# Guard loads five steps ahead, squares on two engines, and head 0 prepared ahead of attention, in a fused gated block with its gradients

## The chip, the cores and the metric

The kernel runs on one core of a Trainium2 chip. The metric is the device time of one execution in microseconds (us); lower is better. Executions of one kernel agree within a few tenths of a per cent. A ratio to the kernel before comes from runs on the same chip, in alternating rounds. The experiments were run in several sets of rounds, on more than one chip, and the median of before lay between 5482 and 5495 us; so between two changed kernels of different sets the ratios are the better comparison.

Abbreviations in the profile: PE is TensorE's matmuls, PEld its weight loads (they overlap PE), DVE is VectorE, ACT is ScalarE, POOL is GpSimd, SP is SyncE. "SPq" is the queue of transfers issued from SP. L324 is line 324 of that kernel's own file; line numbers of before and after differ for the same statement.

## The reference, cut to what matters

```python
def forward(A_x, A_k_cache, A_v_cache, A_wq, A_wo, B_w_gate, B_w_up, B_w_down):
    xn = layernorm(A_x)                                   # 1 x 2048 x 576
    q = (xn @ A_wq) -> 32 heads of 128                    # K, V: 32 x 2048 x 128, given
    p = softmax(q k^T * 128 ** -0.5)
    s = (p v) -> 2048 x 4096, @ A_wo
    g, u = xn @ B_w_gate, xn @ B_w_up                     # 2048 x 4608
    b = (sigmoid(g) * u) @ B_w_down                       # 2048 x 576
    return A_x + s * silu(b)

out, vjp = jax.vjp(forward, ...)
return (out, *vjp(grad_out))                              # and eight gradients; all bfloat16
```

The kernel runs, in this order: layer norm with the gate and up products (`h = sigmoid(g) * u`, stored to DRAM), the w_down product (h is read back transposed), attention forward and backward for 32 heads, and the weight and input gradients. One more thing runs beside gate and up: the *guard*. It sums the squares of all of K and of wq (84 pieces, 21.5 MB read) to bound the largest score, and sets a flag. The flag selects between two versions of attention, one without the row maximum (`fast`) and one with it. In all runs here the fast one is taken.

## The kernel before

The guard: each piece is loaded by SP into one of two buffers of the pool `gd`, and squared by ACT. One piece is issued for each step of the gate/up loop, from the second column group on.

```python
gp = tc.alloc_tile_pool(name="gd", bufs=2)
...
def guard_k(h, hf):
    v = gp.tile([P, GQ], bf, name="gk")
    src = A_k_cache[0, h].rearrange("(p t) d -> p t d", t=NT)[:, hf * NT // 2:(hf + 1) * NT // 2, :]
    nc.sync.dma_start(v[:].rearrange("p (t d) -> p t d", d=P), src)
    nc.scalar.activation(v[:], v[:], AF.Square, accum_out=ksq[:, 2 * h + hf:2 * h + hf + 1])
...                                             # guard_w: the same for pieces of wq
def guard_end():
    ...                                         # sums by partition, into gm
    nc.sync.dma_start(gd_d[0:1, :].rearrange("o p -> p o"), gm[:, 0:1])
    nc.sync.dma_start(gd_d[1:2, :].rearrange("o p -> p o"), gm[:, 1:2])
    gr = gp.tile([1, 2, P], f32, name="gr", bufs=1)
    nc.sync.dma_start(gr[:], gd_d[:, :].rearrange("(o a) p -> o a p", o=1))
    ...                                         # DVE: gs and flag_i from gr
```

The gate/up loop; a step is one pass of the inner loop. `x_all` holds x, then the normalised x, and is dead once it is stored to `xn_d` in the first column group.

```python
for grp in range(NFC // GRP):                   # 3 groups of 3 column chunks of 512
    for st in range(NT):                        # 16 row tiles of 128
        if grp == 0 and st + LA < NT:
            ln_tile(st + LA)
        if grp == 0 and st == NT - 1:
            nc.gpsimd.dma_start(xn_d[:, :].rearrange("(t p) d -> p t d", p=P), xn_st[:])
            ...
        for c in range(GRP):
            ...                                 # 5 + 5 matmuls of 512 columns: g_ps, u_ps
            nc.scalar.activation(a_row[:, cs], g_ps[:], AF.Sigmoid)
            oma = tmpp.tile([P, FCH], bf, name="oma")
            nc.scalar.activation(oma[:], g_ps[:], AF.Sigmoid, scale=-1.0)
            if grp > 0 and guards:
                guards.pop(0)()
            nc.vector.tensor_tensor(h_row[:, cs], u_ps[:], a_row[:, cs], op=ALU.mult)
            nc.vector.tensor_tensor(b_row[:, cs], h_row[:, cs], oma[:], op=ALU.mult)
        ...                                     # GpSimd stores h_row, a_row, b_row to DRAM
```

The w_down stage begins with a transposing read of h, and attention begins by allocating the head tiles, then the score slabs, then the transposed tiles.

```python
for st in ...:
    hT_st = hp.tile([P, FT, P], bf, name="hT_st")
    nc.sync.dma_start_transpose(hT_st[:], h_d[srows, :])
    ...                                         # matmuls with wd_sb, then silu and its derivative

def attention(fast):
    wst = pool("wst", 1)                        # wq_h, woT_h (two each) and wo_h
    ld2, ld1 = pool("ld2", 2), pool("ld1", 1)   # Kn (two), Vn, KT, VT, QT, dOT, dOn, Qn
    slabp = pool("slab", SLABS)                 # 18 slabs "Pq", 128 x 2048 bf16
    wsneg = None if fast else pool("wsneg", 3)
    wpt = pool("wpt", 7 if fast else 4)         # transposed slabs "PT" and "dST"
    wt, stg = pool("wt", 2), pool("stg", 2)
    ...
    def prep_loads(h):
        ...
        hs.wo_h = wst.tile([P, D], bf, name="wo_h")      # 576 x 2 bytes in each partition
        ...
    def transpose_slab(hs, qt, name):
        T = wpt.tile([P, NT, P], bf, name=name, tag="PT")
        nc.sync.dma_start_transpose(T[:], hs.slabs[qt][:])
        return T
    ...
    heads[0] = prep_loads(0)                    # all of head 0's preparation, before any score
    prep_kt(heads[0]); prep_wot(heads[0]); ...
```

Each head has 16 query tiles, and each of them is transposed twice (P for P·V, dS for dQ): 1024 transfers of 512 KB by way of the DMA engines.

Of the kernel before, what the change touches and what calls it, by code (L numbers as in the profile page):

```python
# [13 lines left out]
P = 128  # L14
# [81 lines left out]
def kernel(  # L96
# [67 lines left out]

    px = tc.alloc_tile_pool(name="px", bufs=1)
# [3 lines left out]
    with tc.tile_pool(name="pa", bufs=1) as pa:  # L169
# [7 lines left out]
        NGW = -(-HD // GQ)  # L177

        def guard_k(h, hf):
            v = gp.tile([P, GQ], bf, name="gk")  # L180
            src = A_k_cache[0, h].rearrange("(p t) d -> p t d", t=NT)[:, hf * NT // 2:(hf + 1) * NT // 2, :]
            nc.sync.dma_start(v[:].rearrange("p (t d) -> p t d", d=P), src)
            nc.scalar.activation(v[:], v[:], AF.Square, accum_out=ksq[:, 2 * h + hf:2 * h + hf + 1])

        def guard_w(i, c):
            d0, kd = dts[i]
            n = min(GQ, HD - c * GQ)
            v = gp.tile([P, GQ], bf, name="gk")
            nc.sync.dma_start(v[:kd, :n], A_wq[d0:d0 + kd, c * GQ:c * GQ + n])
            nc.scalar.activation(v[:kd, :n], v[:kd, :n], AF.Square, accum_out=wsq[:kd, NGW * i + c:NGW * i + c + 1])  # L190

# [17 lines left out]
        guards = [lambda h=h, hf=hf: guard_k(h, hf) for h in range(H) for hf in range(2)] + [lambda i=i, hf=hf: guard_w(i, hf) for i in range(DT) for hf in range(NGW)]  # L209
        with tc.tile_pool(name="a1w", bufs=1) as wp:  # L210
            a0x = tc.alloc_tile_pool(name="a0x", bufs=1)
            x_all = a0x.tile([P, NT, D], bf, name="x_all")
# [20 lines left out]
            with tc.tile_pool(name="a0", bufs=3) as sb0, tc.tile_pool(name="a0ps", bufs=2, space=PSUM) as ps0, \  # L233
# [23 lines left out]
                for grp in range(NFC // GRP):  # L257
                    for st in range(NT):
# [9 lines left out]
                        for c in range(GRP):  # L268
# [14 lines left out]
                            if grp > 0 and guards:  # L283
                                guards.pop(0)()
# [6 lines left out]
            a0x.release()  # L291
        for g_ in guards:
            g_()
        guard_end()
        gp.release()
# [4 lines left out]
        with tc.tile_pool(name="a2h", bufs=4) as hp, \  # L300
# [4 lines left out]
            for sg in range(NT // SG):  # L305
# [7 lines left out]
                for sl in range(SG):  # L313
                    st = sg * SG + sl
                    srows = slice(st * P, (st + 1) * P)
                    hT_st = hp.tile([P, FT, P], bf, name="hT_st")
                    nc.sync.dma_start_transpose(hT_st[:], h_d[srows, :])
# [21 lines left out]

            for (t_, sl_, st_) in pend2:  # L340
                transpose_to(nc, pst, t_[:, sl_, :], D, dsT, st_ * P, ident, alt)

    NTH = max(1, NT // 2)
    GPI = -(-NT // NTH)
    SKEW = 5
    G4 = min(4, NT)

    def attention(fast):
        with ExitStack() as es:
            def pool(name, bufs, **kw):  # L350
                return es.enter_context(tc.tile_pool(name=("f_" if fast else "g_") + name, bufs=bufs, **kw))
            wst = pool("wst", 1)
            ld2, ld1 = pool("ld2", 2), pool("ld1", 1)
# [9 lines left out]
            wqs = [wst.tile([P, DT, P], bf, name=f"wq_h{b}") for b in range(2)]  # L363
            woTs = [wst.tile([P, DT, P], bf, name=f"woT_h{b}") for b in range(2)]
            for t_ in wqs + woTs:
                zpad(t_)

            def acc_tile(dtype=f32):
                if dtype == f32:
                    return ps_acc.tile([P, 4, P], f32, name="acc", tag="acc")  # L370
                return ps_acc.tile([P, 8, P], bf, name="acct", tag="acc")

            def pe_transpose_blocks(src_fn, lo, hi, dst_fn, eng):
                for g in range(lo, hi, 8):
                    n = min(8, hi - g)
                    pt = acc_tile(bf)
                    for j in range(n):
                        nc.tensor.transpose(pt[:, j, :], src_fn(g + j), ident[:])
                    alt.copy(dst_fn(g, n), pt[:, :n, :], eng=eng)

            class HeadState:
                pass

            def prep_loads(h):
                hs = HeadState()
                hs.h = h
                hs.wq, hs.woT = wqs[h % 2], woTs[h % 2]
                hcols = slice(h * P, (h + 1) * P)
                nf = DT - 1 if KPAD else DT
                if nf:  # L390
                    nc.gpsimd.dma_start(hs.wq[:, :nf, :], A_wq[:nf * P, hcols].rearrange("(i p) c -> p i c", p=P))
                if KPAD:
                    nc.gpsimd.dma_start(hs.wq[:kd_last, nf, :], A_wq[nf * P:, hcols])
                hs.wo_h = wst.tile([P, D], bf, name="wo_h")
                nc.gpsimd.dma_start(hs.wo_h[:], A_wo[hcols, :])
                hs.Kn = ld2.tile([P, NT, P], bf, name="Kn")
                nc.gpsimd.dma_start(hs.Kn[:], A_k_cache[0, h].rearrange("(p t) d -> p t d", t=NT))
                hs.Vn = ld1.tile([P, NT, P], bf, name="Vn")
                nc.gpsimd.dma_start(hs.Vn[:], A_v_cache[0, h].rearrange("(p t) d -> p t d", t=NT))
                hs.rs_all = hstat.tile([P, NT], f32, name="rs_all")  # L400
                hs.rinv_all = hstat.tile([P, NT], f32, name="rinv_all")
                hs.delta = hstat.tile([P, NT], f32, name="delta")
                hs.negdelta = hstat.tile([P, NT], f32, name="negdelta")
                hs.rsc = hstat.tile([P, NT], f32, name="rsc")
                hs.slabs = [None] * NT
                hs.PT = [None] * NT
                hs.dST = [None] * NT
                return hs

            def prep_kt(hs):  # L410
                hs.KT = ld1.tile([P, S], bf, name="KT")
                KTv = hs.KT[:].rearrange("p (t q) -> p t q", q=P)
                pe_transpose_blocks(lambda j: hs.Kn[:, j, :], 0, NT, lambda g, n: KTv[:, g:g + n, :], "s")

            def prep_vt(hs):
                hs.VT = ld1.tile([P, S], bf, name="VT")
                VTv = hs.VT[:].rearrange("p (t q) -> p t q", q=P)
                pe_transpose_blocks(lambda j: hs.Vn[:, j, :], 0, NT, lambda g, n: VTv[:, g:g + n, :], "v")

            def prep_wot(hs):  # L420
                pt = acc_tile(bf)
                for i, (d0, kd) in enumerate(dts):
                    nc.tensor.transpose(pt[:kd, i, :], hs.wo_h[:, d0:d0 + kd], ident[:])
                nf = DT - 1 if KPAD else DT
                if nf:
                    alt.copy(hs.woT[:, :nf, :], pt[:, :nf, :], eng="s")
                if KPAD:
                    alt.copy(hs.woT[:kd_last, nf, :], pt[:kd_last, nf, :], eng="s")

            def gen_T(w, srcT, dst, sc, eng):  # L430
                acc = acc_tile()
                av = acc[:].rearrange("p a b -> p (a b)")
                cs = slice(sc * CH, (sc + 1) * CH)
                for i, (d0, kd) in enumerate(dts):
                    kk = kfull(i, kd)
                    nc.tensor.matmul(av[:, :CH], lhsT=w[:kk, i, :], rhs=srcT[:kk, i, cs], start=(i == 0), stop=(i == DT - 1))  # L436
                alt.copy(dst[:, cs], av[:, :CH], eng=eng)

            def prep_qt(hs, sc):
                if sc == 0:  # L440
                    hs.QT = ld1.tile([P, S], bf, name="QT")
                gen_T(hs.wq, xnT, hs.QT, sc, "s")

            def prep_dot(hs, sc):
                if sc == 0:
                    hs.dOT = ld1.tile([P, S], bf, name="dOT")
                    hs.dOn = ld1.tile([P, NT, P], bf, name="dOn")
                gen_T(hs.woT, dsT, hs.dOT, sc, "v")

            def prep_don(hs, sc):  # L450
                pe_transpose_blocks(lambda j: hs.dOT[:, j * P:(j + 1) * P], sc * nb, (sc + 1) * nb,
                                    lambda g, n: hs.dOn[:, g:g + n, :], "v")

            def prep_qn(hs):
                hs.Qn = ld1.tile([P, NT, P], bf, name="Qn")
                pe_transpose_blocks(lambda j: hs.QT[:, j * P:(j + 1) * P], 0, NT, lambda g, n: hs.Qn[:, g:g + n, :], "v")
# [18 lines left out]
            def main1(hs, qt, hf):  # L475
                if hf == 0:
                    hs.slabs[qt] = slabp.tile([P, S], bf, name="Pq")
                    hs.rsp = stat.tile([P, NHF], f32, name="rsp")
                    hs.nm = stat.tile([P, NHF], f32, name="nm")
                    hs.snegs = []  # L480
# [101 lines left out]
            NSC = S // CH  # L582
            nb = CH // P

# [29 lines left out]
            def plan(h):  # L614
# [3 lines left out]
                if h:  # L618
                    put(pl + q(skew + 1), 0, lambda: heads.__setitem__(h, prep_loads(h)))
# [27 lines left out]

            heads[0] = prep_loads(0)
            prep_kt(heads[0])
            prep_wot(heads[0])  # L650
            for sc in range(NSC):
                prep_qt(heads[0], sc)
# [278 lines left out]
```

## Time and profile before

Three runs had a median of 5479.09 us (5476.99 to 5485.14). The profiled execution was a slower one of the kernel: its span is 5498.0 us. In this table and the later ones a stage ends where its last instruction starts, and the gradients at the end of the span.

| stage (profile) | ends at, us | length, us |
|---|---|---|
| layer norm, gate and up, guard: to the last of its matmuls | 417.8 | 417.8 |
| gap to the first w_down matmul | 435.4 | 17.6 |
| w_down | 585.5 | 150.1 |
| gap to the first score matmul | 606.2 | 20.7 |
| attention: to the last sum of dK (DVE, behind its last product) | 3903.0 | 3296.8 |
| gradients | 5498.0 | 1595.0 |

This is the page of the kernel before: span, busy time of each engine with its share of the span and its instruction count, and the DMA queues with packets, MB and the share of 16 engines' time.

```profile
span 5498.0 us, 129982 instructions
...
PE 5095.5 (93%) x54343; PEld 3654.3 (66%) x55220; DVE 2497.0 (45%) x5692; ACT 2695.0 (49%) x4794; POOL 1420.1 (26%) x2361
...
q1 hardware_dynamic: 2637890, 764.83, 76.0%
```

PE leads with 93%, so what can be gained is PE's idle time and little else. The average hides the stages. The next lines are the windows view of before: stretch in us, its length, each engine's busy us with instruction counts, the granted TensorE clock (PEclk, 1.00 is full speed), the DMA share and GB/s.

```profile
core 0: us, PE busy (x) PEld busy (x) DVE busy (x) ACT busy (x) POOL busy (x), PEclk, DMA share, GB/s
155.00:291.00 136.00, 108.31 (x475) 47.63 (x485) 54.21 (x98) 100.17 (x195) 26.54 (x50) 0.99 0.66 234
372.00:419.00 47.00, 45.95 (x210) 20.74 (x212) 24.15 (x43) 23.67 (x44) 11.95 (x23) 1.00 0.43 178
700.00:3700.00 3000.00, 2841.93 (x36169) 2259.92 (x36751) 1703.53 (x3814) 1950.09 (x3299) 931.93 (x1600) 1.00 1.14 198
```

With guards (first line) PE is busy 108 of 136 us; without them (second line) 46 of 47. In attention (third line) the DMA share is 1.14. A share above 1 says that the recorded packet times sum to more than the engines' time, so they overlap; I take it as engines that have little time to spare.

The waits view of before, first from 120 to 340 us, then from 340 to 420: who waited for whom, us in total, times, longest.

```profile
ACT gk L183 <- DMA gk<-in_A_k_cache_dram: 46.8, 23, 3.7
PE g_ps L276 <- ACT oma L282: 47.8, 24, 7.5
...
DVE gs L203 <- DMA gr<-gd_d: 10.6, 1, 10.6
PE u_ps L279 <- DVE h_row L285: 8.9, 1, 8.9
```

ACT's squares stand for the guard's loads, the sigmoids stand behind the squares in ACT's order, and PE stands for the sigmoids. Later DVE stands 10.6 us for the guard's sum to return from DRAM, and PE 8.9 us behind DVE. The two gaps are in the timeline view of PE in before (start, length, line, operation; in brackets the idle time ahead and what ended it):

```profile
435.44 17.77 PE L324 MATMUL acc<-wd_sb,hT_st 128*128 128x512 bf16 x125 [17.29 <-DMA hT_st<-h_d]
...
598.11 1.86 PE L378 MATMUL acct<-ident,Kn 128*128 128x128 bf16 x16 [7.48 <-DMA Kn<-in_A_k_cache_dram]
...
606.24 0.59 PE L466 MATMUL sp<-KT,QT 128*128 128x512 bf16 x2
```

```profile
q1 hardware_dynamic: 1942260, 489.69, 100.3%
q0 software_dynamic: 34432, 100.08, 13.3%
```

PE stands 65.6 + 25.6 = 91.2 us of attention for transposed tiles that have not landed. Each packet of the transposing queue takes 3000 us x 16 x 1.003 / 1942260 = 24.8 ns.

### The profile page before, as it was taken

The page shows a single profiled execution, that of the slowest core. Times are in us where ns is not written, and L with a number is a line of the kernel's source. Part 1 is how long each engine was busy: PE and PEld are TensorE (multiplying, and loading weights), DVE is VectorE, ACT ScalarE, POOL GpSimd, SP SyncE. Part 2 cuts the span into 40 slices and gives each one's busy share as a digit, 9 for nine tenths or more (in the row PEclk, how much of TensorE's full clock was granted, in tenths as well). Part 3 has the DMA queues.
Part 4 walks back from the last instruction along what each step waited for, and adds up shares of the span by engine and source line. Part 5 has one row for each costly group of instructions (what it writes and reads, how often), then busy time and mean ns, then how long its engine had stood idle before and what let it go on. Part 6 is the DMA issues. An engine that isn't in the chain of part 4 may idle for free. (4 is left out here: it accounts for less than half of the span.)

```text
span 5498.0 us, 129982 instructions
## 1 busy us (share of the span) xinstructions
PE 5095.5 (93%) x54343; PEld 3654.3 (66%) x55220; DVE 2497.0 (45%) x5692; ACT 2695.0 (49%) x4794; POOL 1420.1 (26%) x2361
## 2 busy tenths in 40 slices
PE   8878899999999999999999999999789999899999
PEld 3334577777777777777777777777557777644454
DVE  4443455655655555655556555555333333210011
ACT  7751466666666666666666666666222222100000
POOL 2212323323333233333233233223112222211000
PEclk9999999999999999999999999999999999999999
DMA  7658799999999999999999999999945455674865
GB/s 282 235 187 194 155 199 189 204 196 201 200 200 198 200 198 193 200 205 199 201 200 199 188 199 198 200 198 189 236 143 195 167 174 180 199 219 120 172 146 111
DMA packets 2721787, 1053.95 MB, mean 192 GB/s; under 512 B 2521937, under 2 KB 2642386, under 8 KB 2719138
## 3 DMA queue, kind: packets, MB, share of 16 engines
q1 hardware_dynamic: 2637890, 764.83, 76.0%
q0 software_dynamic: 83296, 280.64, 16.6%
q8 instruction: 434, 7.11, 0.5%
q14 instruction: 167, 1.37, 0.1%
HBM read 213.91 MB, written 201.00 MB: 75 GB/s over the span
## 5 line engine op out<-in xcount | busy, mean ns | idle before, releaser
L484 ACT ACTIVATE Pq<-sp 128x1024 bf16<-128x1024 f32 x1024 | 1048.1, 1024 | 328.2 <-PE sp L466 205.5
L570 PEld LDWEIGHTS <-Pq 128*128 128x128 bf16 x16384 | 1002.5, 98 | 241.2 <-issue 2.1
L542 ACT ACTIVATE t<-dp,negdelta 128x1024 bf16<-128x1024 f32 x512 | 571.5, 1116 | 278.9 <-POOL negdelta L524 160.7
L538 DVE SCALAR_TENSOR_TENSOR Pq<-dp,delta,Pq 128x1024 bf16<-128x1024 f32 x512 | 655.0, 1279 | 58.1 <-PE acc L510 56.4
L510 PE MATMUL acc<-Kn,dST 128*128 128x128 bf16 x8192 | 554.0, 220 | 69.3 <-DMA dST<-Pq 65.6
L510 PEld LDWEIGHTS <-PT 128*128 128x128 bf16 x8192 | 498.8, 98 | 156.4 <-DMA PT<-Pq 47.8
L543 DVE TENSOR_TENSOR Pq<-t,Pq 128x1024 bf16<-128x1024 bf16 x512 | 419.1, 819 | 398.1 <-ACT t L542 394.9
L535 PE MATMUL dp<-VT,dOT 128*128 128x512 bf16 x1728 | 541.5, 380 | 53.7 <-DVE Pq L538 53.6
L510 PEld LDWEIGHTS <-dST 128*128 128x128 bf16 x8192 | 490.4, 98 | 140.3 <-DMA dST<-Pq 85.7
L510 PE MATMUL acc<-Vn,PT 128*128 128x128 bf16 x8192 | 547.8, 219 | 33.0 <-DMA PT<-Pq 25.6
L570 PE MATMUL acc<-dOn,Pq 128*128 128x128 bf16 x8192 | 546.5, 219 | 10.3 <-DVE o_n L50 0.2
L466 PE MATMUL sp<-KT,QT 128*128 128x512 bf16 x1762 | 547.7, 379 | 1.2 <-ACT Pq L484 1.2
L570 PE MATMUL acc<-Qn,Pq 128*128 128x128 bf16 x8192 | 541.3, 219 | 3.4
L499 POOL TENSOR_SCALAR dOn<-dOn,rinv_all 128x128 bf16<-128x128 bf16 x512 | 313.9, 613 | 612.0 <-DVE rinv_all L472 502.9
L552 ACT ACTIVATE dq_n<-acc,rsc 128x128 bf16<-128x128 f32 x512 | 188.3, 368 | 401.8 <-PE acc L510 401.8
L800 PEld LDWEIGHTS <-xn_all 128*128 128x128 bf16 (+1 forms) x2880 | 281.5, 100 | 40.3 <-issue 11.1
L50 DVE TENSOR_SCALAR o_n<-acc,rinv_all 128x128 bf16<-128x128 f32 x352 | 123.5, 351 | 299.3 <-PE acc L510 299.3
L580 POOL DMA_DIRECT2D out_dram<-kvo x256 | 148.9, 582 | 406.3 <-DVE kvo L579 404.0
L276 PE MATMUL g_ps<-wg_sb,xnT 128*128 128x512 bf16 x694 | 185.8, 392 | 59.8 <-ACT oma L282 50.2
L504 POOL DMA_DIRECT2D dq_d<-dq_n x128 | 98.3, 768 | 497.5 <-ACT dq_n L552 479.7
L535 PEld LDWEIGHTS <-dOT 128*128 128x128 bf16 x2048 | 164.3, 98 | 83.0 <-issue 61.0
L881 ACT ACTIVATE dxn<-acc 128x512 f32<-128x512 f32 (+1 forms) x32 | 12.7, 411 | 420.8 <-PE acc L872 420.8
(182 smaller groups left out, 7163.6 us busy)
## 6 DMA issues: line engine op xcount, KB each, us to landing
out_dram<-kvo POOLq DMA_DIRECT2D x256, 128.0 KB, 4.6
h_d<-h_row POOLq DMA_DIRECT2D x48, 384.0 KB, 4.3
a_d<-a_row POOLq DMA_DIRECT2D x48, 384.0 KB, 3.1
b_d<-b_row POOLq DMA_DIRECT2D x48, 384.0 KB, 5.2
a_blk<-a_d SPq DMA_DIRECT2D x18, 1024.0 KB, 5.8
b_blk<-b_d SPq DMA_DIRECT2D x18, 1024.0 KB, 18.9
h_blk<-h_d POOLq DMA_DIRECT2D x18, 1024.0 KB, 11.4
du_d<-du_blk POOLq DMA_DIRECT2D x18, 1024.0 KB, 9.1
```

The costliest lines, as they stand in the source:

```text
L276: nc.tensor.matmul(g_ps[:], lhsT=xnT[:kk, i, srows], rhs=wg_sb[:kk, i, fs], start=(i == 0), stop=(i == DT - 1))
L466: nc.tensor.matmul(sp[:, c * CH:(c + 1) * CH], lhsT=hs.QT[:, qt * P:(qt + 1) * P], rhs=hs.KT[:, hf * HW_ + c * CH: hf * HW_ + (c + 1) * CH ...
L484: nc.scalar.activation(Pq[:, hsl], sp[:], AF.Exp, scale=SCALE, accum_out=hs.rsp[:, hf:hf + 1])
L499: nc.gpsimd.tensor_scalar(hs.dOn[:, qt, :], hs.dOn[:, qt, :], hs.rinv_all[:, qt:qt + 1], None, op0=ALU.mult)
L510: nc.tensor.matmul(hs.acc[:, 0, :], lhsT=T[:, kt, :], rhs=rhs[:, kt, :], start=(kt == 0), stop=(kt == NT - 1))
L535: nc.tensor.matmul(dp[:, c * CH:(c + 1) * CH], lhsT=hs.dOT[:, qt * P:(qt + 1) * P], rhs=hs.VT[:, hf * HW_ + c * CH: hf * HW_ + (c + 1) * C ...
L538: nc.vector.scalar_tensor_tensor(Pq[:, hsl], dp[:], hs.delta[:, qt:qt + 1], Pq[:, hsl], op0=ALU.subtract, op1=ALU.mult)
L542: nc.scalar.activation(t[:], dp[:], AF.Identity, bias=hs.negdelta[:, qt:qt + 1], scale=1.0)
L543: nc.vector.tensor_tensor(Pq[:, hsl], t[:], Pq[:, hsl], op=ALU.mult)
L552: nc.scalar.activation(hs.dq_n[:, qt % G4, :], hs.acc[:, 0, :], AF.Copy, scale=hs.rsc[:, qt:qt + 1])
L570: nc.tensor.matmul(self.tile[:, j, :], lhsT=self.slabs[qt][:, kt * P:(kt + 1) * P], rhs=self.rhs[:, qt, :], start=(qt == self.lo), stop=(q ...
L800: nc.tensor.matmul(acc[:kd, :], lhsT=xn_all[:, st, d0:d0 + kd], rhs=blk_[:, st, :], start=(st == 0), stop=(st == NT - 1))
```

## The change

Its intent: give the guard's loads a long lead, share the squares between ACT and DVE, and take the two gaps away.

- The guard's pieces go to nine slots of the dead x buffer. A piece is loaded five guard steps before it is squared. Odd pieces are squared on ACT and even ones on DVE.
- The first two transposed h tiles also go to the x buffer, so that they are loaded before the last matmuls of gate and up free their pool.
- Head 0's loads, K^T, wo^T and Q^T are done in the w_down stage. For that the head tiles move out of attention's pools into the pool `pdT`, which lies on the right-hand side of SBUF and lives longer. `hT_st` has three buffers in place of four.

```diff
-        def guard_k(h, hf):
-            v = gp.tile([P, GQ], bf, name="gk")
-            ...
-            nc.scalar.activation(v[:], v[:], AF.Square, accum_out=ksq[:, 2 * h + hf:2 * h + hf + 1])
+        NGS = NT * D // GQ
+        GLA = min(5, NGS - 1)
+        ...
+        def piece_view(k):
+            kind, i, c = pieces[k]
+            v = x_flat[0][:, (k % NGS) * GQ:(k % NGS + 1) * GQ]
+            ...
+        def guard_square(k):
+            v, acc = piece_view(k)
+            if k % 2:
+                nc.scalar.activation(v, v, AF.Square, accum_out=acc)
+            else:
+                nc.vector.scalar_tensor_tensor(v, v, 1.0, v, op0=ALU.mult, op1=ALU.mult, accum_out=acc)
+        ...
+        def guard_step():
+            k = gk[0]
+            if k < len(pieces):
+                guard_load(k)
+            if 0 <= k - GLA < len(pieces):
+                guard_square(k - GLA)
+            gk[0] += 1
 ...
-                            if grp > 0 and guards:
-                                guards.pop(0)()
+                            if grp > 0:
+                                guard_step()
 ...
+            for st in range(NHV):                          # NHV is 2
+                nc.sync.dma_start_transpose(hT_first[st], h_d[st * P:(st + 1) * P, :])
 ...
+        wqs = [pdT.tile([P, DT, P], bf, name=f"wq_h{b}") for b in range(2)]
+        woTs = [pdT.tile([P, DT, P], bf, name=f"woT_h{b}") for b in range(2)]
+        ...
+        wo_h = pdT.tile([P, D], bf, name="wo_h")
+        Kns = [pdT.tile([P, NT, P], bf, name=f"Kn{b}") for b in range(2)]
+        Vn, dOn, Qn = [pdT.tile([P, NT, P], bf, name=nm) for nm in ("Vn", "dOn", "Qn")]
+        KT, VT, QT, dOT = [pdT.tile([P, S], bf, name=nm) for nm in ("KT", "VT", "QT", "dOT")]
+        heads_pre[0] = prep_loads(0)
-        with tc.tile_pool(name="a2h", bufs=4) as hp, \
+        with tc.tile_pool(name="a2h", bufs=3) as hp, \
 ...                                                       # at the end of the w_down stage:
+            prep_kt(heads_pre[0])
+            prep_wot(heads_pre[0])
+            for sc in range(S // CH):
+                prep_qt(heads_pre[0], sc)
 ...                                                       # in attention:
-            wst = pool("wst", 1)
-            ld2, ld1 = pool("ld2", 2), pool("ld1", 1)
             slabp = pool("slab", SLABS)
 ...
-            heads[0] = prep_loads(0)
-            prep_kt(heads[0])
-            prep_wot(heads[0])
-            ...
+            heads[0] = start_head(0)                       # takes what was prepared
```

## The prediction

> **What bounds the kernel now.** PE is busy 93% (page, part 1). Stages (windows view): gate/up 0–419 us, h·w_down 436–586, attention 608 to about 4120, gradients. Only the first two and the seams behind them change.
>
> Gate/up in the timeline: a step (5+5 matmuls of 512 columns) takes 2.16 us at 372–419, where no guard runs. At 155–291 one step with one guard takes 2.8 us (8.4 us a row tile): in the waits, ACT's squares stand 46.8 us for guard loads (two buffers), and the sigmoids behind them hold PE (47.8 us). PE is busy 108 of 136 us there, DMA 66%. The guard's round trip through DRAM then holds DVE 10.6 us and PE 8.9. Seams: PE waits 17.3 us for the first transposed h tile (418–435.4), and from the last w_down matmul (585.7) to the first score matmul (606.2) 20.5 us pass, 7.5 of them a wait for head 0's K.
>
> **The change.** The 84 guard pieces keep their bytes (21 MB). The load lookahead goes from 2 buffers to 9 slots of x, half the squares move from ACT (1.06 us + 0.19) to DVE (I estimate 1.2 us from the 0.76 us of a 576-column scalar_tensor_tensor). Removed from the seams: the h wait, head 0's loads and the idle behind them. Head 0's preparation moves before the branch, not saved. Otherwise attention's built instruction order is the same on PE, DVE, ACT and SP.
>
> The built order decides more than the source: all 84 pieces in 37 steps (2.27 a step, 42 on each engine), starting at step 39 (about 122 us), and then 68 steps without guards. There PE needs 80 us, ACT about 80, DVE about 90 (estimates from durations). DMA needs more: 21.2 MB of guards at 327 GB/s plus 14.2 MB of stores at 411 GB/s (rates: bytes over share of each queue in the DMA view) make 100 us of all 16 engines. The Trainium skill ("Trainium Kernel Development and Optimization", Key Constraints) says that the queues all run on the same 16 engines; here the two queues' shares do add up, 36.6% + 27.7% at 120–340 us. So I expect this burst DMA-bound: about 105 us.
>
> **Sum** (estimates). Gate/up: 122 + 3 (first guard load waits for the store of x, 10.9 us to landing) + 105 + 68 × 2.16 + 6 (the guard's DRAM round trip is still in DVE's order 2–3 steps after its start) = about 383 instead of 419: −36. h seam: 17 to about 1: −16. Attention seam: KT, woT and Q (about 7 us at warm clock) run while the last ds tile is made, first score matmul about 10 us after the last w_down matmul: −10. Together −62: **5417 us**, 8 in 10: 5392 to 5444. Chances: faster by over 2% 0.03, within 2% 0.96, slower 0.01.
>
> **What would show it.** Gate/up ends near 383; DMA share over 0.9 for some 100 us from about 125; DVE waiting on the guard's returning load 6–10 us; first w_down matmul within 2 us of the last gate/up step; first score matmul 10 us after the last w_down matmul; attention and later stages within 5 us of before.
>
> **What would make it wrong.** DMA carries more than 340 GB/s in the burst: up to 25 us better. Guard waits on two in-order engines stall PE more, or stores pile up: 20 us worse. The head-0 loads delay the third h tile. Attention, 64% of the span, shifting.

## More of the kernel before

In attention two groups of the page carry the waits (L510: busy us, mean ns, then idle us just before, and its main releaser), and the DMA view from 700 to 3700 us gives the queue that carries the transposes (q1: packets, MB, share):

```profile
L510 PE MATMUL acc<-Kn,dST 128*128 128x128 bf16 x8192 | 554.0, 220 | 69.3 <-DMA dST<-Pq 65.6
...
L510 PE MATMUL acc<-Vn,PT 128*128 128x128 bf16 x8192 | 547.8, 219 | 33.0 <-DMA PT<-Pq 25.6
```

## The result, and the profile after

| | median, us | runs |
|---|---|---|
| before | 5482.11 (5476.99 to 5492.95) | 4 |
| after | 5346.53 (5345.28 to 5347.66) | 4 |

The ratio is 0.975, with a 95% interval of 0.9733 to 0.9767: faster by 2.5%. Here and below a ratio is the mean time of one kernel's fast runs over that of the other's of the same rounds, so it is not quite the ratio of the medians quoted. The gain of 136 us is more than twice the 62 us of the prediction, and the time lies below its range.

| stage (both profiles) | before, us | after, us | difference | predicted |
|---|---|---|---|---|
| gate and up | 417.8 | 378.6 | -39.2 | -36 |
| gap to w_down | 17.6 | 1.4 | -16.2 | -16 |
| w_down | 150.1 | 148.1 | -2.0 | 0 |
| gap to attention | 20.7 | 7.1 | -13.6 | -10 |
| attention | 3296.8 | 3213.2 | **-83.6** | within 5, with the gradients |
| gradients | 1595.0 | 1595.1 | +0.1 | |
| span | 5498.0 | 5343.5 | -154.5 | -62 |

The profiled execution of before was 16 us slower than its median, so the sum of differences is larger than the 136 us between medians. The page of the kernel after, the same lines:

```profile
span 5343.5 us, 129930 instructions
...
PE 5067.8 (95%) x54343; PEld 3653.5 (68%) x55220; DVE 2540.5 (48%) x5776; ACT 2649.6 (50%) x4710; POOL 1415.3 (26%) x2361
...
q1 hardware_dynamic: 2637890, 764.83, 71.7%
```

ACT has 84 instructions fewer and DVE 84 more: each of the 42 squares that moved is a pair of instructions. The last line is the surprise: the same packets and the same MB as before, to the digit, but a share that is 4.3 points smaller, and of a shorter span. The windows view of after, with the burst of guards, the stretch without them, and attention:

```profile
122.00:228.00 106.00, 82.98 (x351) 35.54 (x358) 82.12 (x154) 80.87 (x157) 18.37 (x34) 0.97 0.90 326
243.00:379.00 136.00, 133.95 (x603) 60.48 (x614) 71.80 (x132) 67.88 (x125) 33.53 (x63) 0.99 0.56 197
630.00:3630.00 3000.00, 2896.23 (x37084) 2320.61 (x37680) 1751.19 (x3924) 1993.39 (x3377) 953.40 (x1644) 1.00 1.04 203
```

The guards now come as a burst of about 106 us at a DMA share of 0.90, and 150 us without guards follow; in the last 136 of them PE is busy for 134. The attention share fell from 1.14 to 1.04. The DMA view of the burst, 125 to 228 us, shows both queues:

```profile
q1 hardware_dynamic: 11274, 20.45, 57.8%
q0 software_dynamic: 2640, 12.98, 31.9%
```

The Trainium skill ("Trainium Kernel Development and Optimization", Key Constraints) says that all issuing queues run on the same 16 DMA engines and interleave. The view counts both queues as shares of the same engines (57.8 + 31.9 = 89.7%), so this sum alone is no test. The packet records of after are in keeping with it: from 630 to 3630 us a 256-byte packet of the SP queue took 47.9 ns in the mean where a packet of the POOL queue was under way at its start, and 18.9 ns elsewhere. The waits view of after, from 118 to 232 us, then from 228 to 380:

```profile
PE g_ps L377 <- ACT oma L383: 22.6, 16, 2.4
ACT x_all L277 <- DMA x_all<-in_A_k_cache_dram: 22.3, 13, 6.7
...
DVE gs L304 <- DMA gr<-gd_d: 8.8, 1, 8.8
PE u_ps L380 <- DVE h_row L386: 5.2, 1, 5.2
```

The chain from load to square to sigmoid to PE is halved, not gone. The return of the guard's sum still holds DVE. The timeline view of PE in after:

```profile
377.70 1.24 PE L380 MATMUL u_ps<-wu_sb,xnT 128*128 128x512 bf16 x5
...
380.00 17.80 PE L439 MATMUL acc<-wd_sb,x_all 128*128 128x512 bf16 x141 [1.06 <-DVE h_row L386]
...
528.16 1.06 PE L176 MATMUL pt<-ident,Kn 128*128 128x128 bf16 x16
...
535.23 0.61 PE L514 MATMUL sp<-KT,QT 128*128 128x512 bf16 x2
```

Both gaps shrank as intended, from 17.6 to 1.4 us and from 20.7 to 7.1. The windows view shows one more gain: in before the granted clock was 0.51 to 0.56 from 422 to 440 us and 0.52 from 590 to 604 us, in and just behind the gaps; in after it is 1.00 from 380 to 384 and from 528 to 535 us. Four microseconds at 0.56 of the clock lose about 1.8 us (an estimate from these figures), which is most of the 2.0 us that w_down became shorter. Attention, which the change was not meant to touch, is the largest part of the gain. The two groups of the page of after, and the DMA view of after from 630 to 3630 us:

```profile
L558 PE MATMUL acc<-Kn,dST 128*128 128x128 bf16 x8192 | 551.4, 219 | 3.6
...
L558 PE MATMUL acc<-Vn,PT 128*128 128x128 bf16 x8192 | 546.7, 219 | 7.0
```

```profile
q1 hardware_dynamic: 1988572, 501.37, 91.4%
q0 software_dynamic: 35344, 102.83, 11.6%
```

The 91.2 us in which PE stood for transposed tiles are gone: the waits view of after has no such line. A packet of the transposing queue takes 3000 x 16 x 0.914 / 1988572 = 22.1 ns, where it took 24.8. So the same transfers became cheaper by a tenth in a stage whose DMA share was above 1.

### The profile page after: what moved, and what is told of

Read it like the earlier page. It is cut to its first block, busy times and chain, and to the rows that moved or that the text cites. A ratio compares the mean times of both kernels' runs of the same rounds, so it can differ in the third digit from the quotient of the medians.

```text
span 5343.5 us, 129930 instructions
## 1 busy us (share of the span) xinstructions
PE 5067.8 (95%) x54343; PEld 3653.5 (68%) x55220; DVE 2540.5 (48%) x5776; ACT 2649.6 (50%) x4710; POOL 1415.3 (26%) x2361
## 4 chain that ended last, share of the span: by engine, by line
PE 82%; issue 4%; DMA 2%; DVE 2%; SPq 2%; ACT 1%; POOL 1%; ACTq 0%; DVEq 0%; POOLq 0%
PE acc L618 16%; PE acc L558 15%; PE acc L913 7%; PE sp L514 7%; PE accw L841 6%; PE dp L583 6%; PE acc L223 5%; PE dh L818 3%; PE accq L881 3%; PE acc L872 2%; PE acct L176 2%; PE acc L439 2%; PE accd L830 2%; PE acc L780 2%; DMA out_dram<-kvo 2%
## 5 line engine op out<-in xcount | busy, mean ns | idle before, releaser
L586 DVE SCALAR_TENSOR_TENSOR Pq<-dp,delta,Pq 128x1024 bf16<-128x1024 f32 x512 | 655.1, 1279 | 34.0 <-PE acc L558 32.0
L519 DVE TENSOR_REDUCE rs_all<-rsp 128x1 f32<-128x2 f32 x512 | 78.2, 153 | 291.9 <-ACT Pq L532 289.6
```

Source lines behind the costliest of these rows:

```text
L586: nc.vector.scalar_tensor_tensor(Pq[:, hsl], dp[:], hs.delta[:, qt:qt + 1], Pq[:, hsl], op0=ALU.subtract, op1=ALU.mult)
```

## The experiments

### Where the question stood

The built order of attention's instructions is the same in both kernels on every engine, apart from head 0's preparation; the order in the two traces agrees. So something other than order had to make the transposes cheaper. One thing that the change moved is addresses. In the compiled programs the tiles of the fast attention start at these byte offsets in their partitions:

```
                        before          after
slabs Pq (18 x 4096)    80512 ...       37376 ...
PT/dST (7 x 4096)       154240 ...      111104 ...
first slab mod 256      128             0
first PT/dST mod 256    128             0
```

In before, the tile `wo_h` (576 x 2 = 1152 bytes, four and a half times 256) lies ahead of the slabs and shifts everything behind it by half of 256. In after it has moved to the other side of SBUF. The trace's packet records, counted over the same 3000 us as the DMA views, give a mean of 25.03 ns for 256-byte packets in before, with 14.0% of them over 18 ns, and 22.26 ns and 2.6% in after (the 24.8 and 22.1 ns above divide a whole queue's share by its packets, and differ a little for that). The median is 18 ns in both: most packets cost the same, and more of them are slow in before.

Theory: the address of the transposes' source slabs sets the cost of a packet, and this is what shortened attention. Rivals: (1) attention benefits from the earlier preparation or from another phase between the engines; (2) the destination tiles' address is what counts; (3) the slow packets of before come from contention with the other queue. Against the third, the trace itself: of the packets that started while no packet of the other queue was under way (86% of all in before, 88% in after), 13.8% took over 18 ns in before and 2.3% in after. The same address could also cost the engines that read and write the slabs. Their instructions show none of it: the mean of ACT's writing of a slab is 1024 ns in before and in `b_align` below, and that of DVE's product on it 1279 and 1280 ns.

Every kernel below gave the correct result, apart from `a_half`, whose guard sees half its data on purpose.

### b_align: before, with the slabs on a multiple of 256

```diff
+            pool("padA", 1).tile([P, 64], bf, name="padA")       # 128 bytes, unused
             slabp = pool("slab", SLABS)
```

> The kernel before with one change: a 128-byte tile that nothing uses in front of the slabs, so that slabs and transposed tiles start at a multiple of 256 bytes of their partition instead of 128 beyond one. Instruction orders are those of before. Theory A (start address of the tiles that the DMA transposes touch): attention, first score matmul to last dK store, falls from 3297 us to about 3215, total about 5400, the waits of PE for transposed tiles vanish, packets over 18 ns in attention fall from 15% to under 5%. Rival B (head 0's prepared tiles and tiles kept over heads relax waits, or attention starts in another phase): total stays at 5480 within 10 us.

Measured: 5412.83 us (5407.11 to 5413.57, 4 runs) against 5486.72 us for before in the same rounds (7 runs); ratio 0.9866 (0.9846 to 0.9886). In its profile gate and up end at 418.3 us, as in before, and attention takes 3209.8 us. The page and the DMA view of `b_align` from 700 to 3700 us:

```profile
L511 PE MATMUL acc<-Kn,dST 128*128 128x128 bf16 x8192 | 551.2, 219 | 3.6
```

```profile
q1 hardware_dynamic: 1989868, 501.70, 91.2%
```

One unused tile of 128 bytes takes 74 us off the kernel before, with no other part of the change. The packets are at 22.0 ns, 2.6% of the 256-byte ones take over 18 ns, and PE's waits for transposed tiles are gone. Rival 1 falls: nothing is prepared earlier here.

### a_mis: after, with everything from the slabs on moved by 128 bytes

```diff
+            pool("padA", 1).tile([P, 64], bf, name="padA")
             slabp = pool("slab", SLABS)
```

> The changed kernel with the same 128-byte tile in front of the slabs, which puts slabs, transposed tiles and all after them 128 bytes beyond a multiple of 256. Theory A: attention back to about 3297 us, total about 5430 (5346 + 84). Rival B: total stays at 5346 within 10 us.

Measured: 5420.65 us (5413.12 to 5425.11, 4 runs); ratio 0.9886 (0.9866 to 0.9905). Attention takes 3275.1 us. The page and the DMA view of `a_mis` from 630 to 3630 us:

```profile
L559 PE MATMUL acc<-Kn,dST 128*128 128x128 bf16 x8192 | 554.9, 220 | 53.8 <-DMA dST<-Pq 50.3
```

```profile
q1 hardware_dynamic: 1953119, 492.43, 100.8%
```

The same pad gives back 74 us of the change (10 less than the expectation took from the profile of before, and attention is 3275 us and not 3297). The four kernels form a square: the pad is worth 74 us without the change's other parts (`b_align`) and 74 with them (`a_mis`), and the other parts are worth 66 us at either address (5486.72 - 5420.65 = 66.1, and 5412.83 - 5346.53 = 66.3). The 5346.53 us of after come from an earlier set of rounds, in which before was 5 us faster. By the ratios, which allow for that, the pad is worth 1.34 and 1.36% (74 and 75 us), and the other parts 1.14 and 1.16% (63 and 64 us). So the two causes add up, and neither depends on the other within what these runs resolve. The profiles, single executions, scatter more: between them the pad changes attention by 87 us (before and `b_align`) and by 62 (after and `a_mis`).

### a_src and a_dst: source alone, destination alone

```diff
 a_src
+            pool("padA", 1).tile([P, 64], bf, name="padA")
             slabp = pool("slab", SLABS)
+            pool("padB", 1).tile([P, 64], bf, name="padB")       # back to a multiple of 256
             wsneg = None if fast else pool("wsneg", 3)
             wpt = pool("wpt", 7 if fast else 4)
 a_dst
             slabp = pool("slab", SLABS)
+            pool("padA", 1).tile([P, 64], bf, name="padA")
             ...
             wpt = pool("wpt", 7 if fast else 4)
+            pool("padB", 1).tile([P, 64], bf, name="padB")
             wt, stg = pool("wt", 2), pool("stg", 2)
```

(The fast version has no pool `wsneg`.)

> The changed kernel with 128 bytes in front of the slabs and 128 behind them: only the source of the transposes (slabs) stands off, the transposed tiles and everything behind them at multiples of 256. If the read side costs: total about 5430, as with both off. If the write side costs: 5346.

> The changed kernel with 128 bytes between slabs and transposed tiles and 128 behind these: only the destination of the transposes stands off. If the write side costs: total about 5430. If the read side costs: 5346. In the stage before attention transposed h tiles start 32 bytes beyond a multiple of 256 in the changed kernel, and packets are as fast as before, so I expect the read side to cost and this run at 5346.

Measured: `a_src` 5395.29 us (5381.97 to 5406.37, 4 runs), ratio 0.9829 (0.9804 to 0.9854), attention 3273.5 us in its profile. `a_dst` 5350.74 us (5347.66 to 5354.18, 4 runs), ratio 0.9757 (0.9738 to 0.9777), attention 3209.2 us. One line of the page and the DMA view from 630 to 3630 us, for `a_src` and then for `a_dst`:

```profile
L560 PE MATMUL acc<-Kn,dST 128*128 128x128 bf16 x8192 | 555.3, 220 | 58.7 <-DMA dST<-Pq 54.9
...
q1 hardware_dynamic: 1951722, 492.08, 101.9%
```

```profile
L560 PE MATMUL acc<-Kn,dST 128*128 128x128 bf16 x8192 | 551.4, 219 | 3.6
...
q1 hardware_dynamic: 1991536, 502.11, 91.3%
```

The source's address makes the packets dearer, the destination's alone does not. Rival 2 falls. (The h tiles that the expectation of `a_dst` names: 4.3% of their 256-byte packets took over 18 ns in before, 4.0% in after, with means of 19.8 and 20.9 ns in 150 us of w_down.) By the medians `a_src` lost 49 us of the 74 that `a_mis` lost, and the intervals of their ratios do not overlap (at most 0.9854 against at least 0.9866). So some 25 us of `a_mis` (31 by the ratios) go with the tiles behind the slabs being off as well, though moving the transposed tiles alone cost 4 us in `a_dst`. The profiles do not show where: the two agree within 2 us in attention, but the profiled execution was the slowest of `a_src` and the fastest of `a_mis`. This part stays open.

### a_off32 and a_off224: is it the size of the offset?

The Trainium skill ("DMA: Bandwidth & Descriptors", How a descriptor splits into AXI transactions) says that a transaction must start at a 256-byte boundary, that a descriptor which does not start on one begins its first transaction at the boundary below, and that the unused bytes still cost beats of 32 bytes. The page has no example of 256 bytes. Counted by its rule (my estimate, which takes each 256-byte packet record as one descriptor), a packet would take 8 beats at offset 0, and 9, 12 and 15 at offsets 32, 128 and 224. These are the beats that the two expectations below go by. If beats set the cost, offset 32 should be nearly free.

```diff
 a_off32 (a_off224 has 112 and 16 in place of 16 and 112)
+            pool("padA", 1).tile([P, 16], bf, name="padA")       # 32 bytes
             slabp = pool("slab", SLABS)
+            pool("padB", 1).tile([P, 112], bf, name="padB")      # 224 bytes
             wsneg = None if fast else pool("wsneg", 3)
```

> The changed kernel with the slabs 32 bytes beyond a multiple of 256 (32 bytes in front, 224 behind, so the transposed tiles are at a multiple). [...]I expect a small cost: packets at 22 to 23.5 ns, attention within 20 us of 3213. If any offset costs the same: attention at about 3275 as with 128, total about 5400.

> The same with the slabs 224 bytes beyond a multiple of 256[...]. If beats count: slower than 128 off, packets over 26 ns, attention over 3300, total over 5430. If any offset costs the same: about 5400.

| slabs at (mod 256) | kernel | median, us | ratio (95%) | attention, us | mean packet, ns |
|---|---|---|---|---|---|
| 0 | after | 5346.53 | 0.975 (0.9733 to 0.9767) | 3213.2 | 22.26 |
| 32 | a_off32 | 5418.96 | 0.985 (0.9815 to 0.9886) | 3281.2 | 25.05 |
| 128 | a_src | 5395.29 | 0.9829 (0.9804 to 0.9854) | 3273.5 | 25.29 |
| 224 | a_off224 | 5403.19 | 0.9831 (0.9799 to 0.9862) | 3277.8 | 25.24 |

The DMA view of `a_off32` from 630 to 3630 us:

```profile
q1 hardware_dynamic: 1949164, 491.42, 100.9%
```

The expectation of a nearly free offset 32 was wrong: any offset costs the same within the scatter (the medians come from different chips; the intervals of the three ratios overlap). The direction of the page's rule agrees with the runs, the beats that I counted by it do not order them. Nor did every packet become dearer: the median is 18 ns at all four offsets, and what grows is the share over 18 ns, from 2.6% to 13.4 to 14.7%. By the page's rule the number of transactions (two in place of one) is the same at all three offsets; that would fit, but no run shows that this is the mechanism.

### a_half: what limits the burst of guards?

Theory: the DMA engines, as predicted. Rival: the 84 squares on two engines that work in order. In this kernel every second piece is not loaded; the square of it reads the slot of the piece before, so that all squares stay and half the bytes go.

```diff
-            v = x_flat[0][:, (k % NGS) * GQ:(k % NGS + 1) * GQ]
+            v = x_flat[0][:, (k // 2 % NGS) * GQ:(k // 2 % NGS + 1) * GQ]
 ...
-            if k < len(pieces):
+            if k < len(pieces) and k % 2 == 0:
                 guard_load(k)
```

> The changed kernel with every second guard piece not loaded: its square is taken of the piece before, so ACT and DVE do all 84 squares and only the bytes of the guard are halved (the guard sees half of K and wq on purpose; the flag, and so the outputs, stay). If the guard burst is held by DMA: its 37 steps shrink from 106 us towards 85, gate/up ends near 358 instead of 379. If the two in-order engines hold it: it stays at about 106 us.

Measured: one run, 5320.79 us (state unknown, so its total is not compared). In its trace the squares start from 124.2 to 206.6 us, where in after they start from 121.8 to 227.8, so the burst shrank from 106 to 82 us; gate and up end at 357.5 us, 21 us earlier than in after. The windows view of `a_half` over the same stretch as above:

```profile
122.00:228.00 106.00, 97.22 (x434) 42.70 (x433) 91.31 (x180) 89.01 (x172) 22.75 (x42) 0.97 0.80 267
```

With all squares in place and half the bytes, PE is busy 97 of the 106 us where it was 83 (the last 21 us of this window lie behind the burst). So the guard's loads set the pace of the burst in after, and not the squares; `a_half` halves their bytes and their number together, and does not part the two. It also shows the next limit: in the 85 us from 122 to 207 DVE is busy 82.0 and ACT 80.4, close to the 90 and 80 that the prediction estimated for them.

### a_best, a_defer, a_best2, a_best3: spreading the bytes

If the burst is limited by bytes, its loads should be spread over more steps. The built order had put the 84 squares into 37 steps, though the source asks for one a step: the engines' orders are set by the scheduler. `a_best` ties each guard step behind its sigmoid and its product, starts it earlier by storing `xn_d` two row tiles earlier, and moves DVE's work on the guard's returning sum into the w_down stage. `a_defer` has this last part alone.

```diff
 a_best: pacing
-                        if grp == 0 and st == NT - 1:
+                        if grp == 0 and st == NT - 1 - LA:
                             nc.gpsimd.dma_start(xn_d ...
 ...
-                            nc.scalar.activation(oma[:], g_ps[:], AF.Sigmoid, scale=-1.0)
-                            if grp > 0:
-                                guard_step()
-                            nc.vector.tensor_tensor(h_row[:, cs], u_ps[:], a_row[:, cs], op=ALU.mult)
+                            ia = nc.scalar.activation(oma[:], g_ps[:], AF.Sigmoid, scale=-1.0)
+                            iv = nc.vector.tensor_tensor(h_row[:, cs], u_ps[:], a_row[:, cs], op=ALU.mult)
+                            if grp > 0 or st > NT - 1 - LA:
+                                with tc.issue_after(ia.ins), tc.issue_after(iv.ins):
+                                    guard_step()
 a_best and a_defer: from the load of gr on, guard_end becomes a function of its own
+        def guard_flag(gp):
             gr = gp.tile([1, 2, P], f32, name="gr", bufs=1)
             ...
             acc_box[0] = a2_acc
+            guard_flag(sb)
 a_best2: a_best, and five guard steps in four steps of the loop
+                                    if (st * GRP + c) % 4 == 0:
+                                        guard_step()
 a_best3: a_best2, and the reading of gr ordered behind the last product of the w_down stage
-            guard_flag(sb)
+            with tc.issue_after(last_v.ins):     # last_v: the product that makes ds_t
+                guard_flag(sb)
```

> The changed kernel with the squares held to one a step in the scheduler's order (each is told to stand behind the sigmoid or the product of its step), so the same guard bytes spread over 84 steps instead of 37, and with the guard's returning load taken in the stage after gate/up. If the burst is DMA-bound and the round trip costs 5 to 8 us: gate/up ends near 350 instead of 379, total about 5317. If the burst isn't the limit: total within 8 us of 5346.

> As a_best, with five squares in four steps, so the guard ends some 17 steps earlier (about 280 us) and the two early transposed h tiles are asked for before the last third of the row stores, as in the changed kernel. If in a_best the h tiles came late because they waited for the last squares: no wait for the first h tile (a_best: 7.1 us), gate/up still ending near 347 us, total 5310 to 5318. If the h tiles collide with the row stores whenever they come: again about 5328.

> The changed kernel with the guard's returning load and its five small DVE instructions taken in the stage after gate/up, nothing else. If the DRAM round trip costs gate/up what its waits say: gate/up ends 5 to 7 us earlier (379 to about 373), total about 5341. If PSUM buffers hide it: no change.

> As a_best2, but DVE's reading of the guard's returning load is told to stand behind the last product of the second stage, where the load has landed long before. In a_best2 and in the changed kernel with the load deferred, DVE stood 14 to 17 us for it in the second stage and PE 5 to 7 us behind DVE. If that was the whole reason why deferring brought nothing: that wait vanishes, the second stage is 5 to 8 us shorter, total 5306 to 5313 against 5317 of a_best2. If not: 5317.

| kernel | median, us | ratio (95%) | gate and up end, us |
|---|---|---|---|
| after | 5346.53 (4 runs) | 0.975 (0.9733 to 0.9767) | 378.6 |
| a_defer | 5357.63 (1 run, state unknown) | | 373.8 |
| a_best | 5328.1 (4 runs) | 0.9706 (0.9668 to 0.9744) | 345.1 |
| a_best2 | 5316.75 (4 runs) | 0.9677 (0.9651 to 0.9704) | 344.6 |
| a_best3 | 5310.85 (5 runs) | 0.9675 (0.9653 to 0.9697) | 341.9 |

`a_best` took 33 us out of gate and up, but only 18 us out of the time (by the medians; after is of another set of rounds, and by the ratios it is 24). The waits view of `a_best` from 340 to 390 us shows where part of it was given back:

```profile
PE acc L442 <- DMA x_all<-h_d: 7.1, 1, 7.1
...
PE acc L442 <- DMA hT_st<-h_d: 3.1, 1, 3.1
```

In `a_best` the squares are still going on late in gate and up, and the first h tiles, which share the x buffer with the guard, are loaded beside the last row stores. They landed late. In all, the w_down stage of `a_best` is 171.1 us long in its profile, against 148.1 in after: PE's idle time is one part, and its granted clock another, 0.76 from 380 to 400 us and 0.87 from 400 to 420, where after has 1.00. `a_best2` ends the guards some 17 steps sooner, and this wait is gone. Its own waits view from 340 to 390 us names the next one:

```profile
DVE gs L306 <- DMA gr<-gd_d: 17.0, 1, 17.0
...
PE pt L59 <- DVE ds_t L453: 7.4, 1, 7.4
```

The deferred wait for the guard's sum had only been moved: it stood in DVE's order early in the w_down stage, and PE stood behind it. `a_defer` shows the same by itself: gate and up ended 5 us earlier, and DVE then waited 14.3 us in the w_down stage. Its one run is not faster than after, and its attention happened to be 14 us longer, so the time of that run decides nothing. `a_best3` orders the reading behind the stage's last product. The wait for `gr` is no longer in its waits, and it is the fastest of all: 5310.85 us (5303.4 to 5314.6), 36 us below after by the medians, 41 by the ratios. Its own gain over `a_best2` is within the intervals and is not shown. The windows view of `a_best3`:

```profile
122.00:228.00 106.00, 105.48 (x483) 47.98 (x492) 83.94 (x155) 81.33 (x154) 26.88 (x50) 1.00 0.94 332
```

PE is busy 105.5 of 106 us at a DMA share of 0.94: the bytes now go through beside the matmuls and not in their place. The squares are spread from 134 to 276 us here.

## Why the prediction was wrong

**What bounds the kernel: right.** PE's idle time was the thing to gain. The profiled span fell by 154.5 us and PE's busy time by only 28 us (5095.5 to 5067.8), so 127 us of it was idle time of PE.

**Gate and up: right.** Predicted to end near 383, measured 378.6. The burst was predicted at about 105 us from about 125, DMA-bound, with a share over 0.9; it ran from 122 to 228 at 0.90, and `a_half` shows that the loads limit it. The square on DVE was estimated at 1.2 us and took 1.217. DVE's wait for the returning sum was predicted at 6 to 10 us and was 8.8.

**The gap to w_down: right.** Predicted -16 us, measured -16.2.

**The gap to attention: right in mechanism, a little small.** Predicted -10 us, with the first score matmul 10 us after the last of w_down; it came 7.1 us after, for -13.6.

**Guards and gaps together: right.** The 62 us of the sum compare with the 66 us (63 by the ratios) that `a_mis` and `b_align` isolate at equal addresses.

**Attention: wrong, and this is the step that failed.** The prediction says "attention and later stages within 5 us of before". It rested on the sentence that "attention's built instruction order is the same on PE, DVE, ACT and SP". That sentence is true, and it was not enough. The step from the same order to the same time left out that the change also moves the tiles, and that here the mean of the transposing packets depends on their source's address (25.03 ns against 22.26). Attention became 84 us shorter in the profile; `b_align` and `a_mis` put the effect of the addresses at 74 us of run time. The source slabs alone bring 49 of these (`a_src`), the destination alone 4 (`a_dst`); the rest is not placed. The profile of before had shown where to look: a DMA share of 1.14 and 91 us of PE standing for transposed tiles. Here a tenth off the packets' mean time went with the loss of all 91 us of these waits.

**The risks: named, and not weighed.** "Attention, 64% of the span, shifting" stands among the things that would make it wrong, yet faster by over 2% got a chance of 0.03 only. (The prediction lets attention end at about 4120 us; by the last sum of dK it ends at 3903, and is 60% of the span.) A change that reorders the pools of a stage with a DMA share above 1 should have had a wider range, or a look at the addresses, which the compiled program shows before any run.

## What to carry to other kernels

Where a stage's DMA share is at or above 1 and PE waits for transposed tiles, look up the start addresses of the transposes' source tiles modulo 256 before and after any change to pools: one tile of 1152 bytes ahead of them cost this kernel 74 us, and an unused tile of 128 bytes took it back. When a change moves allocations, judge the stages that it "does not touch" by their addresses as well as by their instruction order. Spread a load that is limited by bytes over the built order and not over the source's, and when a wait is deferred, check where the waiting instruction now stands in its engine's order, or the wait only moves.

## What the Trainium skill lacked or had wrong

- "DMA: Bandwidth & Descriptors", DMA Transpose (X-bar), Constraints, lists a 32-byte alignment in SBUF and no other. Slabs at 32, 128 and 224 bytes past a multiple of 256 meet that, give correct results, and cost 60 to 68 us of attention against slabs on a multiple of 256 (3273.5 to 3281.2 us against 3213.2). The page could say that for SBUF-to-SBUF transposes like these (128 x 2048, bf16) a source that starts at a multiple of 256 bytes was faster. With the source on a multiple, a destination 128 bytes off left attention as it was (3209.2 us).
- The same page, How a descriptor splits into AXI transactions: misaligned descriptors do cost more, as it says, but the beats that follow from its rule (9, 12 and 15 at offsets 32, 128 and 224, by my count) do not order the runs, which have mean packets of 25.05, 25.29 and 25.24 ns against 22.26 at offset 0. That a packet record is one descriptor is assumed.
- No page that I read names the way this comes about: a tile of 1152 bytes ahead of other pools moves all their tiles off a multiple of 256 (80512 = 314 x 256 + 128 in the program before).
- No page that I read says how to take a DMA share above 1 where the transfers stay within SBUF; here 1.14 went with 91 us of PE standing for transfers, and 1.04 with none on the same instructions.
